# A state-space scan and four gated experts on one core: all tokens in four blocks of six chunks, each with fifteen products for eighteen

## The chip, the cores and the metric

The kernel runs on one core of a Trainium2 chip. A core has TensorE (called PE in the profile; its weight loads are PEld), VectorE (DVE), ScalarE (ACT), GpSimd (POOL) and SyncE (SP), whose queue issues nearly all transfers here. The metric is the time of one execution on the device in microseconds (us); the time before is the median of three runs, 623.88 us (623.67 to 624.11). A profile is one further execution, and its span is what the profiler saw between the first and the last instruction.

## The reference, cut to what matters

Two parts follow one another. The first is a chunked scan with a decaying state for 4 sequences of 768 tokens with 8 heads; the second mixes four experts (each two matrix products with a ReLU between) by gates per token.

```python
# first part, per sequence and head (C, B: 16 states; x: 32 values)
cum = np.cumsum(log_a_chunk)
L = np.exp(cum[:, None] - cum[None, :]) * causal
y = (C @ B.T * L) @ x + (C @ state) * np.exp(cum)[:, None]
state = np.exp(sum(log_a_chunk)) * state + (B * decay_from_j).T @ x
# bridge: y of all heads side by side gives 3072 tokens x 256
# second part
p = domain_probs / domain_probs.sum(-1, keepdims=True)
for e in range(4):
    h = np.maximum(x @ w1[e], 0.0)      # w1[e]: 256 x 1024
    out += p[:, e:e + 1] * (h @ w2[e])  # w2[e]: 1024 x 256
```

All is in 32-bit floats. The second part is most of the work.

## The kernel before, in words

The 3072 tokens are 24 chunks of 128. The first part turns each pair of chunks into a tile `yT` (features down, 256 tokens across, two halves of 128 features). The hidden units are 16 slices `fb` of 256, four to each expert. In the second part the unit of work on TensorE is a *product* (`product`, L860): two matmuls of 128x128 weights against 128x256 values, added up in half a PSUM bank or across its two halves. Done plainly, one slice and one pair of chunks take two products in the first layer and two in the second.

The kernel spares products by the family of schemes known from fast matrix multiplication: sums of weights times sums of tokens. Two are in the code, as tables at L301 to L326. `B` treats two weight slices and two pairs of chunks (a block of four chunks) with seven products for eight in each layer (`twos_first`, L1004). `H` treats three slices and three pairs (a block of six chunks) with fifteen products for eighteen (`threes_first`, L1038); as 16 slices are five groups of three and one over, one slice in a block of six is done plainly. `ORDER` (L326) lists the blocks: three of `B`, two of `H`. In block 0 the four slices of the first expert are done plainly in the first layer, so that work can start before sums exist.

What a saved product costs elsewhere:
- Sums of weights, `operands` (L920): raw slices come from HBM into W tiles; additions at L955 (DVE or POOL) make the sums, which L960 also stores in `w_d`, so that a later block reloads them (L952) instead of adding again.
- Sums of tokens, `token_sums` (L964): 256-wide additions on DVE into Y tiles.
- Between the layers: `snap` (ScalarE copies a bank to a V tile), `seed` (ScalarE copies a V tile into a bank, on which PE then adds up), `combine` (L885, an addition on DVE, or on POOL where both inputs are in SBUF) and `gated` (L896, DVE: ReLU and gate in one instruction). `threes_right` (L1080) and `twos_right` make the right-hand sums for the second layer.
- The second layer, `second` and `visit`, adds up its products in "houses", half banks that keep their sums from unit to unit: seeded, added to, copied out (L1124). At the end of a block `result` (L1159) adds them into the output, `leave` stores it.

A *unit* of the program is one group of slices (three for `H`, two pairs of slices for `B`). Its first-layer products are interleaved one for one (`put`) with the second-layer products of the unit before it (`behind`). Into this line the first part of the next block's chunks is set: scores (L472), scans of decays (`decays`, L748), outputs (L796) and `carry`, at the places that `PAIRS_AT` names, "s1" for the scores of pair 1, "o12" for the outputs of pairs 1 and 2.

The instruction order of TensorE is thus given by hand. The order on all other engines is made by a small list scheduler in the file, `Plan.run` (L181). It knows a nominal duration for each operation (`D512`, `D256` and literals), gives each a latest time from its users on TensorE, picks per engine what is ready and most urgent, chooses between DVE and POOL for additions (`BACK`, `SLACK`), keeps buffers back for urgent work (`KEEP`) and decides which buffer of a kind (V, W, Y, bank ...) a value lives in. `EARLY` lists the units in which the weight sums for the blocks of six are made ahead of time, on POOL alone (`due` in `operands`), and stored. `NV` and `NW` count the V and W tiles.

Ahead of all that, up to L692, the first two chunks are worked by hand: their decays, scores, outputs, the gates, and the first weight loads.

Of the kernel before, what the change touches and what calls it, by code (L numbers as in the profile page):

```python
# [19 lines left out]
D512, D256 = .64, .36  # L20
LANDING = 2.2
KEEP = 5
NV, NW = 31, 28
SLACK, BACK, YIELD = 0.0, 3.0, 6.0
EARLY = 1, 2, 3, 4, 5, 6, 7, 8, 9, 10
SOFT = 1
ROUND = 0, 3, 2, 0, 4
RATE, MARGIN = 330.0, 2.0
AFTER = 1
HOLD = 12.0  # L30
# [4 lines left out]
SCORED = 4  # L35
HELD = ("x", "w"), (5, 8), (0, 7)
# [6 lines left out]
    (3, 2): ((0, 1, "s0"), (1, 5, "s1"), (1, 24, "o01")),  # L43
    (4, 2): ((0, 1, "s0"), (2, 1, "s1"), (2, 14, "o01")),
    (4, 3): ((0, 1, "s0"), (0, 14, "o0"), (1, 1, "s1"), (2, 1, "s2"), (2, 14, "o12")),
    (6, 3): ((0, 1, "s0"), (0, 14, "o0"), (2, 1, "s1"), (3, 1, "s2"), (3, 14, "o12")),
# [28 lines left out]
class Plan:  # L75
# [105 lines left out]
    def run(self, line, at, begin):  # L181
# [19 lines left out]
        while todo:  # L201
# [4 lines left out]
            for w in waiting[e]:  # L206
                if w.start is not None or e == "PE" and w.place != head:
                    continue
                ready = max([w.ready, w.after.nominal + late if w.after else 0.0] + [
                    n.end + (MARGIN if n.kb and e != "SP" else -n.lag if n.by == e == "PE" else HOP)  # L210
                    for n in w.needs])
                if len(w.on) > 1 and e == "POOL":
                    if max(ready, now) + w.on[e] > w.latest + late + SLACK or self.backlog(
                            waiting["DVE"], now, t["DVE"], w) < BACK:
                        continue
                rank = w.latest
                if e == "DVE" and w.two and self.port > now + 0.05:
                    rank += YIELD
                if best is not None and ready <= now and rank >= best[0]:
                    continue  # L220
                when, homes = self.homed(
                    w, max(now, ready, self.port if e == "POOL" and w.port else 0.0))
                if when is None:
                    continue
                if when <= now + 0.02:
                    if best is None or rank < best[0]:
                        if e == "DVE" and w.two:
                            when = max(when, self.port)
                        best = rank, w, when, homes
                else:  # L230
                    if e == "DVE" and when <= now + NEAR and now < FIRST and (near is None or rank < near[0]):
                        near = rank, when
                    if soon is None or when < soon:
                        soon = when
# [79 lines left out]
H.houses = ((13, 2), (11, 4), (0, 7), (1, 14), (6, 9), (5, 8), (10, 12), (3,), ("x", "w"))  # L314
H.plain = {(0, 0): 7, (1, 0): 0, (1, 1): 8, (1, 2): 5, (0, 1): "x", (0, 2): "w"}
# [9 lines left out]
B.houses = ((1, 2), (3, 7), (5, 6), (4,))  # L325
ORDER = B, B, B, H, H  # L326
# [9 lines left out]
def kernel(  # L336
# [188 lines left out]
    a_sb = const.tile([NCH * NH // 2, 2, P], FP32, name="a_sb")  # L525
# [59 lines left out]
    a_cut = const.tile([NCH * NH // 2, 2, P], FP32, name="a_cut")  # L585
# [45 lines left out]
    gs = some(2, [P, NT, P], "gs")  # L631
# [93 lines left out]
    aq = plan.taken("V", NV - 2, 0.0)  # L725
    for c, i in ((2, 2), (3, 3)):
        st[c]["xb"] = plan.taken("xb", i, now)
# [192 lines left out]
    def operands(k, scheme, fbs, l, after=None, due=None, loaded=()):  # L920
# [3 lines left out]
        for f, fb in enumerate(fbs):  # L924
            v = loaded[f] if loaded else value("W")
            used = {x[1] for r, x in scheme.blocks[l].items() if x[0] == f and r != "b"}
            if loaded:
                pass
            elif len(used) == 1 and (*fbs, l, 0) in w_d:
# [229 lines left out]
    def result(k):  # L1159
# [3 lines left out]
        def acc(r):  # L1163
            for house in scheme.houses:
                if r in house:
                    v, i = kept.get((k, (r,)), kept.get((k, house))), house.index(r)
                    return v, lambda: whole(v)[:, i * FB:i * FB + FB]
# [22 lines left out]
        if scheme is B:  # L1190
            u, u7, u5, _ = pieces(2)
# [4 lines left out]
                     (0, 1): (acc(3), 1, u5), (1, 1): (acc(5), 1, u7)}  # L1196
        else:
# [90 lines left out]
    twos = [tuple(fbs[i:i + 2]) for i in range(0, EPB, 2)]  # L1288
    for two in twos:
        operands(0, B, two, 2, loaded=[weights[0, fb, 2] for fb in two])  # L1290
    line.extend(second(0, [(two, {1: h[two[0], 0], 2: h[two[1], 0]}) for two in twos], [(1, 2)]))
    for c in range(4):
        carry(c)
    units, last_made = [], {}
    for k, b in enumerate(blocks):
        n = E if b.scheme is B else NG
        lead = ROUND[k]
        for g in [*range(lead, n), *range(lead)]:
            if b.scheme is B and (k or g):
                units.append((k, [(4 * g + i, 4 * g + i + 1) for i in (0, 2)]))  # L1300
            elif b.scheme is H:
                units.append((k, [(3 * g + 1, 3 * g + 2, 3 * g + 3)]))
        if b.scheme is H:
            units.append((k, None))
# [14 lines left out]
    for fb in fbs:  # L1319
        first[fb, 1], h[fb, 1] = plain_first(0, fb, 1)  # L1320
    line.extend(x for fb in fbs for x in first[fb, 1])
    token_sums(0)
    right = [(two, {r: v for r, v in twos_right({
        (f, n): h[fb, n] for f, fb in enumerate(two) for n in range(2)}).items() if r > 2}) for two in twos]
    behind = second(0, right, B.houses)
# [3 lines left out]
    for u, (k, groups) in enumerate(units):  # L1329
# [28 lines left out]
        else:  # L1358
            held = [(fbs, right(h)) for fbs, (_, h) in zip(groups, made)], b.scheme.houses
# [8 lines left out]
        if k < len(blocks) - 1:  # L1368
            for unit, x, what in PAIRS_AT[len(of_block), blocks[k + 1].scheme.pairs]:
# [13 lines left out]
                at[x] = line[mark:]  # L1383
# [58 lines left out]
```

## Time and profile before

| what | value |
|---|---|
| median of 3 runs | 623.88 us (623.67 to 624.11) |
| the profiled execution | 624.43 us, of which its span 622.5 us |
| PE busy | 617.0 us (99%), 3435 records |
| PEld busy | 528.5 us (85%) |
| DVE busy | 531.3 us (85%), 883 instructions |
| ACT busy | 268.3 us (43%), 568 |
| POOL busy | 172.3 us (28%), 199 |
| DMA | 126.65 MB, mean 203 GB/s |

How to read it: an engine's busy time is what its instructions cover, and says nothing yet about who waits for whom. A row of forty digits cuts the span into equal slices, each digit the busy share in tenths. The chain follows the last instruction back to what released it, again and again, to the start; an engine with a large share of it sets the time. A group line names the source line, engine, operation, the tiles by the program's names, how often, then busy time and the mean of one in ns, then the engine's idle time before those instructions and what ended it. Each fp32 matmul of the program leaves two records. A query by stretches gives busy time and counts of each engine between two moments of the span.

### The profile page before, as it was taken

The numbers are of one execution on the slowest core, as the hardware profiler recorded it, in microseconds if no ns is written. First come the engines' busy times: TensorE is split into PE (matmuls) and PEld (weight loads), VectorE is DVE, ScalarE is ACT, GpSimd is POOL, SyncE is SP. The second block draws the span as 40 slices with busy tenths as digits, with TensorE's granted clock in tenths as the row PEclk, the third lists the DMA queues.
The fourth block names the chain that finished last, engine by engine and source line by source line (L and its number), as shares of the span: only waits on it lengthen the run. The fifth ranks groups of instructions, "written<-read, shape, count | busy, mean of one in ns | idle before, by whom it ended". The sixth has DMA issues, their size and how long they took to land.

```text
span 622.5 us, 10250 instructions
## 1 busy us (share of the span) xinstructions
PE 617.0 (99%) x3435; PEld 528.5 (85%) x3435; DVE 531.3 (85%) x883; ACT 268.3 (43%) x568; POOL 172.3 (28%) x199
## 2 busy tenths in 40 slices
PE   9999999999999999999999999999999999999997
PEld 5888888888888888888888888888888888888886
DVE  7999999997968799789689999959797987869684
ACT  4242464422356343236534336445443344555441
POOL 4637644840527654156350000100000000000000
PEclk9999999999999999999999999999999999999999
DMA  7999489673898878399999737535131424943001
GB/s 253 330 298 359 152 273 276 231 247 88 271 341 291 284 227 264 63 332 322 346 352 292 249 79 255 180 117 178 59 110 52 138 40 122 376 130 111 0 1 51
DMA packets 112307, 126.65 MB, mean 203 GB/s; under 512 B 28916, under 2 KB 78336, under 8 KB 112256
## 3 DMA queue, kind: packets, MB, share of 16 engines
q1 hardware_dynamic: 112100, 125.96, 63.0%
q8 instruction: 27, 0.44, 0.3%
q14 instruction: 24, 0.20, 0.1%
q10 hardware_dynamic: 156, 0.06, 0.0%
HBM read 101.09 MB, written 24.89 MB: 202 GB/s over the span
## 4 chain that ended last, share of the span: by engine, by line
PE 98%; DVE 1%; ACT 0%; issue 0%; DVEq 0%; ACTq 0%
PE bank L864 91%; PE bank L505 2%; PE bank L472 2%; DVE LT L489 1%; PE bank L810 1%; PE bank L644 1%; DVE MT L788 0%; PE bank L620 0%; PE bank L1245 0%; PE bank L612 0%; ACT A L515 0%; ACT v L687 0%; DVE v L1176 0%; ACT v L1250 0%; DVE v L899 0%
## 5 line engine op out<-in xcount | busy, mean ns | idle before, releaser
L864 PE MATMUL bank<-v,w 128*128 128x256 f32 x1856 | 436.6, 380 | 0.0
L864 PEld LDWEIGHTS bank<-v,w 128*128 128x128 f32 x1856 | 351.1, 190 | 51.9 <-issue 3.6
L891 DVE TENSOR_TENSOR v<-v,v 128x512 f32<-128x512 f32 x267 | 196.6, 765 | 16.2 <-ACT v L873 13.5
L864 PE MATMUL bank<-Y,w 128*128 128x256 f32 x792 | 203.3, 379 | 0.0
L864 PEld LDWEIGHTS bank<-Y,w 128*128 128x128 f32 x792 | 150.3, 190 | 20.9 <-issue 0.6
L899 DVE SCALAR_TENSOR_TENSOR v<-bank,gate 128x512 f32<-128x512 f32 x172 | 116.8, 684 | 34.9 <-PE bank L864 30.2
L878 ACT COPY bank<-v 128x512 f32<-128x512 f32 (+1 forms) x195 | 109.0, 571 | 64.4 <-DVE v L891 42.6
L955 POOL TENSOR_TENSOR w<-w,w 128x256 f32<-128x256 f32 x102 | 100.5, 1008 | 55.4 <-PE bank L864 19.6
L873 ACT COPY v<-bank 128x512 f32<-128x512 f32 x106 | 62.0, 585 | 109.3 <-PE bank L864 108.9
L1124 ACT COPY v<-bank 128x512 f32<-128x512 f32 x105 | 61.5, 585 | 96.2 <-PE bank L864 95.0
L891 POOL TENSOR_TENSOR v<-v,v 128x512 f32<-128x512 f32 x11 | 15.6, 1414 | 247.2 <-DVE v L891 192.6
L489 DVE TENSOR_TENSOR_SCAN LT<-ab,ident 128x512 f32<-128x512 f32 x42 | 53.0, 1276 | 0.4 <-DMA ab<-acut_d 0.4
L891 DVE TENSOR_TENSOR v<-bank,v 128x512 f32<-128x512 f32 x40 | 27.6, 689 | 9.1 <-PE bank L864 8.9
L499 POOL TENSOR_TENSOR MT<-xb,LT 128x64 f32<-128x64 f32 (+1 forms) x28 | 16.3, 586 | 42.5 <-DVE LT L489 31.5
L773 POOL TENSOR_TENSOR cts<-ctm,dec 128x256 f32<-128x256 f32 x20 | 17.6, 892 | 37.0 <-ACT ctm L465 24.5
L788 DVE TENSOR_TENSOR MT<-bank,LT 128x512 f32<-128x512 f32 x44 | 27.3, 681 | 0.1
L1127 ACT COPY v<-bank 128x256 f32<-128x256 f32 x22 | 8.2, 372 | 37.8 <-PE bank L864 33.9
L1176 DVE TENSOR_TENSOR v<-v,v 128x256 f32<-128x256 f32 x52 | 20.3, 420 | 4.0 <-ACT v L1124 3.9
L465 ACT ACTIVATE ctm<-xb,tmask 128x128 f32<-128x128 f32 x48 | 16.4, 394 | 15.0 <-DMA xb<-in_xbc_dram 15.0
L1026 DVE TENSOR_TENSOR bank<-bank,v 128x512 f32<-128x512 f32 x22 | 15.2, 693 | 5.2 <-PE bank L864 5.0
L955 POOL TENSOR_TENSOR w<-w 128x256 f32<-128x256 f32 x14 | 14.1, 1008 | 11.8 <-DMA w<-in_w_dram 6.9
L955 DVE TENSOR_TENSOR w<-w,w 128x256 f32<-128x256 f32 x36 | 14.9, 443 | 0.0
(71 smaller groups left out, 202.5 us busy)
## 6 DMA issues: line engine op xcount, KB each, us to landing
w<-w_d SPq DMA_DIRECT2D x134, 256.0 KB
w<-in_w_dram SPq DMA_DIRECT2D x128, 256.0 KB
w_d<-w SPq DMA_DIRECT2D x82, 256.0 KB
ab<-acut_d SPq DMA_DIRECT2D x21, 512.0 KB
w<-in_w_dram SPq DMA_DIRECT2D x40, 128.0 KB
gate<-p_d SPq DMA_DIRECT2D x10, 384.0 KB
xb<-in_xbc_dram SPq DMA_DIRECT2D x17, 192.0 KB
gate<-p_d SPq DMA_DIRECT2D x11, 256.0 KB
```

Of the source, the lines that this page charges most:

```text
L465: nc.scalar.mul(ctm[:, t], xb[:, OCT:OCT + P], tmask[:, t:t + 1])
L489: nc.vector.tensor_tensor_scan(out=LT.rearrange("p h s -> p (h s)")[:, lo:lo + w], data0=src, data1=ident.rearrange("p h s -> p (h s)")[:, ...
L773: plan.add({"POOL": .72}, lambda e: nc.gpsimd.tensor_mul(s["cts"].t, s["ctm"].t, s["dec"].t.unsqueeze(1).to_broadcast([HN, NT, P])), reads ...
L788: nc.vector.tensor_mul(s["MT"].t[:, js, h, 0:P], g, s["LT"].t[:, js, h])
L864: nc.tensor.matmul(out=o, lhsT=w[:, j], rhs=x if half is None else x[:, j], start=(start and j == 0), stop=(j == 1), skip_group_check=True)
L873: act(.5, lambda e: nc.scalar.copy(out=flat(v), in_=bank.t), reads=[bank], writes=[v])
L878: act(.54 if to - lo > FB else .32, lambda e: nc.scalar.copy(out=bank.t[:, lo:to], in_=flat(v)[:, lo:to]), reads=[v], writes=[bank])
L891: plan.add(engines, lambda e: (on(e).tensor_add if sign > 0 else on(e).tensor_sub)(flat(v), whole(x), whole(y)), reads=[x, y], writes=[v], ...
L899: dve(D512, lambda e: nc.vector.scalar_tensor_tensor(out=h.t, in0=whole(x).rearrange("p (j m) -> p j m", j=JJ), scalar=0.0, in1=g.t[:, 2 * ...
L955: plan.add({"POOL": .72} if due else B256, lambda e, r=r, x=x, y=y, sign=sign: (on(e).tensor_add if sign > 0 else on(e).tensor_sub)(view(r ...
L1124: act(.5, lambda e: nc.scalar.copy(out=flat(v), in_=bank.t), reads=[bank], writes=[v])
L1176: plan.add(engines, lambda e: (on(e).tensor_add if sign > 0 else on(e).tensor_sub)(o[1](), x[1](), y[1]()), reads=[v for v in vs if v is n ...
```

## The change

All 24 chunks now go by the scheme `H`: `ORDER` is four blocks of six. With no block of four left, the weight sums can't be made during one: `EARLY` is empty, and each group's sums are made when block 0 (for one group: block 1) first uses the group, on DVE or POOL, and stored; later blocks reload them.

Block 0 begins otherwise. The slices of the first expert are done plainly in both layers and for all three pairs: the first layer of pair 0, its second layer (house (0, 7)), the first layer of pair 1, its second layer (house (8, "x")), with the scores and outputs of chunks 4 and 5 set into and behind these, then pair 2, whose second layer (5, "w") is interleaved with the first unit. Block 0 has then four groups and no plain unit of its own. Its houses are paired a little differently (`first_houses`), which `acc` in `result` takes account of.

Around it: other nominal durations and thresholds for the scheduler, 34 V tiles for 31 and 27 W tiles for 28; the tiles of `a` and of two early score copies (`gs`) are laid into a V and a W tile that are not yet in use; other places in `PAIRS_AT`; the order of groups in a block (`ROUND`); POOL takes no choice additions before 30 us of planned time (`EASY`).

```diff
-D512, D256 = .64, .36
+D512, D256 = .60, .34
-KEEP = 5
-NV, NW = 31, 28
-SLACK, BACK, YIELD = 0.0, 3.0, 6.0
-EARLY = 1, 2, 3, 4, 5, 6, 7, 8, 9, 10
+KEEP = 7
+NV, NW = 34, 27
+SLACK, BACK, YIELD = 0.0, 2.0, 6.0
+EARLY = ()
-ROUND = 0, 3, 2, 0, 4
+ROUND = 0, 4, 3, 2
-HOLD = 12.0
+HOLD = 6.0
+EASY = 30.0
+FOURS = 4
...
-    (4, 3): ((0, 1, "s0"), (0, 14, "o0"), (1, 1, "s1"), (2, 1, "s2"), (2, 14, "o12")),
-    (6, 3): ((0, 1, "s0"), (0, 14, "o0"), (2, 1, "s1"), (3, 1, "s2"), (3, 14, "o12")),
+    (4, 3): ((0, 1, "s0"), (0, 14, "o0"), (1, 1, "s1"), (1, 14, "o1"), (2, 1, "s2"), (2, 14, "o2")),
+    (6, 3): ((0, 1, "s0"), (2, 1, "o0"), (2, 1, "s1"), (3, 1, "s2"), (3, 23, "o12")),
...
-                            waiting["DVE"], now, t["DVE"], w) < BACK:
+                            waiting["DVE"], now, t["DVE"], w) < (BACK if now > EASY else 99):
...
+H.first_houses = ((13, 2), (11, 4), (0, 7), (1, 14), (6, 9), (8, "x"), (5, "w"), (10, 12), (3,))
...
-ORDER = B, B, B, H, H
+ORDER = H, H, H, H
...
-    a_sb = const.tile([NCH * NH // 2, 2, P], FP32, name="a_sb")
+    a_sb, a_cut = (homes["V"][-4][:NCH * NH // 2, i].rearrange("p (r s) -> p r s", r=2) for i in range(2))
...
-    gs = some(2, [P, NT, P], "gs")
+    gs = [homes["W"][-1][:, NT * P * i:NT * P * (i + 1)].rearrange("p (t s) -> p t s", t=NT) for i in range(2)]
...
-    twos = [tuple(fbs[i:i + 2]) for i in range(0, EPB, 2)]
-    for two in twos:
-        operands(0, B, two, 2, loaded=[weights[0, fb, 2] for fb in two])
-    line.extend(second(0, [(two, {1: h[two[0], 0], 2: h[two[1], 0]}) for two in twos], [(1, 2)]))
+    line.extend(visit(0, (0, 7), plain_terms(0, fbs, h, [(0, 0), (1, 0)])))
     for c in range(4):
         carry(c)
+    dma(lambda e: nc.sync.dma_start(
+        out=g0.t[:, 4:6], in_=p_d[0, 4:6].rearrange("c s -> (c s)").partition_broadcast(P).rearrange(
+            "p (c s) -> p c s", s=P)), 1, 128, part=[g0])
+    for c in (4, 5):
+        fetch(c)
+        decays(c)
+    for fb in fbs:
+        first[fb, 1], h[fb, 1] = plain_first(0, fb, 1)
+    begun = [x for fb in fbs for x in first[fb, 1]]
+    line.extend(begun[:FOURS])
+    scores([4, 5])
+    line.extend(begun[FOURS:])
+    line.extend(visit(0, (8, "x"), plain_terms(0, fbs, h, [(1, 1), (0, 1)])))
+    outputs([4, 5])
+    for c in (4, 5):
+        carry(c)
...
-        first[fb, 1], h[fb, 1] = plain_first(0, fb, 1)
-    line.extend(x for fb in fbs for x in first[fb, 1])
+        first[fb, 2], h[fb, 2] = plain_first(0, fb, 2)
+    line.extend(x for fb in fbs for x in first[fb, 2])
     token_sums(0)
-    right = [(two, {r: v for r, v in twos_right({
-        (f, n): h[fb, n] for f, fb in enumerate(two) for n in range(2)}).items() if r > 2}) for two in twos]
-    behind = second(0, right, B.houses)
+    behind = visit(0, (5, "w"), plain_terms(0, fbs, h, [(1, 2), (0, 2)]))
```

Left out of this copy: the loss of the argument `loaded` in `operands`, what the scheme `B` would need as a first block (it isn't used any more), the new `acc`, the note of when the two borrowed tiles come free, and that two things may stand at one place of `PAIRS_AT`.

## The prediction

> **What bounds the kernel now.** I read the page from the top, then the chain, then stages cut at the points where the chain passes a score matmul (L472), then single stretches of the timeline. First the page of before: busy times, the slices, the chain's shares, and the groups that matter.
>
> ```profile
> span 622.5 us, 10250 instructions
> ...
> PE   9999999999999999999999999999999999999997
> ...
> DVE  7999999997968799789689999959797987869684
> ...
> POOL 4637644840527654156350000100000000000000
> ...
> PE 98%; DVE 1%; ACT 0%; issue 0%; DVEq 0%; ACTq 0%
> ...
> L864 PE MATMUL bank<-v,w 128*128 128x256 f32 x1856 | 436.6, 380 | 0.0
> ...
> L864 PE MATMUL bank<-Y,w 128*128 128x256 f32 x792 | 203.3, 379 | 0.0
> ...
> L955 POOL TENSOR_TENSOR w<-w,w 128x256 f32<-128x256 f32 x102 | 100.5, 1008 | 55.4 <-PE bank L864 19.6
> ```
>
> TensorE (PE) is busy in every slice and holds 98% of the chain; its two product groups show no idle time before them. So time goes with the number of products while nothing makes PE wait. But VectorE (DVE) is nearly as full in many slices: it is the next bound.
>
> The chain in order of time gives the price of a product. Columns: start, length, what.
>
> ```profile
> 34.35 1.08 PE bank L472 x16
> 35.43 24.37 PE bank L864 x112
> ```
>
> 112 matmul records in 24.37 us are 0.218 us each; the longest piece of the chain (924 in 199.63 us) gives 0.216. A program matmul leaves two records and a product is two program matmuls, so a product costs 4 x 0.216 = 0.865 us.
>
> Now the stages between score matmuls (columns: stretch, length, then busy time and count of PE, weight loads, DVE, ACT, POOL, then clock, DMA share, GB/s).
>
> ```profile
> 34.35:59.80 25.45, 25.45 (x133) 21.92 (x132) 25.16 (x43) 9.77 (x19) 13.60 (x12) 1.00 0.98 327
> 59.80:108.92 49.12, 49.12 (x324) 42.20 (x324) 47.54 (x86) 24.34 (x58) 24.73 (x29) 1.00 0.74 237
> 108.92:158.54 49.62, 49.62 (x245) 43.20 (x244) 44.54 (x69) 17.59 (x32) 19.88 (x23) 1.00 0.57 180
> ...
> 317.35:371.47 54.12, 54.12 (x305) 46.47 (x304) 51.45 (x86) 21.63 (x48) 6.97 (x8) 1.00 0.71 225
> 371.47:398.64 27.17, 27.17 (x140) 23.44 (x140) 26.01 (x40) 13.24 (x25) 1.59 (x1) 1.00 0.70 227
> ...
> 413.68:615.69 202.01, 202.01 (x940) 177.83 (x940) 164.57 (x284) 92.05 (x176) 3.83 (x3) 1.00 0.35 106
> ```
>
> The reader is to see two kinds of stage in which DVE is 95% or more full and PE still never waits: the early one, where POOL works half the time, and the first block of six (317 to 399), where POOL hardly works. The changed kernel puts the two on top of each other.
>
> [...] Timeline of before, six alike DVE additions with POOL at work and six without:
>
> ```profile
> 83.10 5.12 POOL L955 TENSOR_TENSOR w<-w,w 128x256 f32<-128x256 f32 x5 [0.18 <-PE bank L864]
> ...
> 85.83 4.97 DVE L891 TENSOR_TENSOR v<-v,v 128x512 f32<-128x512 f32 x6
> ...
> 490.57 3.69 DVE L891 TENSOR_TENSOR v<-v,v 128x512 f32<-128x512 f32 x6
> ```
>
> 4.97 against 3.69: the trace agrees that they hinder each other (1.28 us lost to about five POOL operations), though both still progress. I price by the measured loss.
>
> **The change, part by part.**
>
> *Products.* Counted from the instruction orders of both kernels: L864 has 1324 program matmuls before (its 2648 records are twice that), and the same line has 1308 after. By hand: before 114+112+112+162+162 = 662 products, after 168+162+162+162 = 654. Eight fewer, 8 x 0.865 = **-6.9 us**, on the path. Every other matmul line has the same count in both orders.
>
> *Spacing of DVE work.* Start to start without POOL: a 512-wide operation 3.61/6 = 0.60 (490.57 to 494.18), 256-wide 0.34 (two of L955 from 78.73 to 79.40), a decay scan of 512 1.13 (101.41 to 102.54), a dec scan 0.40, a state update 0.6. I count each kernel's DVE instructions between consecutive score products and multiply. Before: the three early stages need 21.9, 41.9 and 38.5, were busy 25.16, 47.54 and 44.54, in sum 14.9 more, with 58.2 us of POOL beside them: 0.25 us lost per busy POOL us (single stages 0.23 to 0.30). The check: 317 to 371 needs 50.1 and was busy 51.45 with 6.97 of POOL.
>
> *Block 0 after.* Plain column pairs, then four groups of fifteen. Between the scores of chunks 4,5 and those of 12,13, PE's own work is 127.8 us (by 0.435 a matmul, and scores, outputs as in the chain). DVE's need by the same counts is 19.9+21.9+27.0+50.7 = 119.5. POOL has some 43 sums of weights (1.008), 8 L773 (0.892), 7 additions of 512 (1.414) and 12 L499 (0.6) there: 67.5 us. At 0.25 that costs DVE 16.9, so DVE needs 136.4 against 127.8: **8.6 us too much**. With 0.20 it is 5.2, with 0.30 12. Of the 32 additions and gates of a group, 13 (threes_right) feed second-layer products which come one unit, about 26 us, later; they can slip, 13 x 0.60 = 7.8 us of work in any unit, as far as the V buffers allow (34 instead of 31). So most of the excess becomes a backlog rather than a wait; gates and seeds of the first layer can't slip. Below nothing it can't go, since PE has no wait here to lose; above, all 8.6 falls on PE. I take a quarter, **+2.1**, with first-unit seeds as the likeliest place: a score multiplication and a scan stand on DVE ahead of the subtraction of product 12, which ScalarE then copies to a bank that PE wants.
>
> *A new wait.* The output matmuls of chunks 4,5 are directly followed by plain products on those outputs. PE's first matmul there waits for ScalarE's copy of chunk 5. Nearest row: the same step of chunk 1.
>
> ```profile
> 12.00 0.51 ACT L687 COPY v<-bank 128x128 f32<-128x128 f32 x2 [0.32 <-PE bank L505]
> ...
> 12.77 0.30 PEld L864 LDWEIGHTS bank<-v,w 128*128 128x128 f32 x2 [0.33 <-ACT v L687]
> ```
>
> 0.32 to the copy, 0.38 for a 128x256 copy (L825 has 376 ns), 0.26 until the weight load: **+1.0 us**, and all queued PE work stands behind it. Between 0.7 and 1.5. Before, eight other products lay at the like place.
>
> *Blocks 1 to 3.* Block 1 makes the last twenty sums: DVE needs 133.8 plus some 11 for 44 us of POOL, against 144.2 of PE. Even, so a backlog isn't worked off there. Blocks 2 and 3 make no sums and are like before's stages from 317 on, where PE never waited: 56.5+24.9 against 87.4, then 163.5 against 222. Nothing added.
>
> *What moves without a price.* Sums fall from 164 to 100 (POOL 116 to 56, DVE 48 to 44) and no longer run ahead of their users: in before POOL did the hundred for the blocks of six long before their use. In block 0 a late one stops PE; each has more than a unit, and is in the excess above. Transfers shrink: 256 KB weight loads 128 to 88, reloads of sums 134 to 110, stores 82 to 50, half loads 40 to 22, gates about equal: some 27 MB less of 126.65. SP's queue is 558 rows against 674; in block 0 it brings six raw tiles per 26 us plus chunks, less than the 327 GB/s of before's fullest early stage. ScalarE gets 29 instructions more (43% busy): hidden. The a rows and the score copies now live in a V and a W buffer that are wanted only after they are free. One W home less: a group takes 16, two groups overlap as in before's blocks of six. The planner's constants (durations nearer to the 0.60 and 0.34 above, KEEP, BACK, HOLD, EASY) add no instruction of their own; what they do to the order is in the counts, which are of the order as it comes out. The end of the program has the same six result transposes.
>
> **Sum**, against the profiled execution (span 622.5, 624.43 with 1.93 around it): 622.5 - 6.9 + 1.0 + 2.1 = 618.7, with the 1.93, 620.6. The median of the runs shown is 0.55 below that execution, so **620.1**.
>
> **Rivals.**
> - *The backlog hides all.* DVE is 96% full in 371.47:398.64 with no PE wait, which speaks for a planner that copes; there POOL was quiet, which speaks against. 624.43 - 6.9 + 1.0 - 0.55 = 618.0, or 617.0 without the new wait.
> - *A wash.* Waits of 5.7 to 8.2 eat the gain: half or more of the excess on PE and the first-unit seeds late by a few us. 622.6 to 625.1, middle 623.9.
> - *Slower: [...].* All the excess falls on PE: 623.88 - 6.9 + 1.0 + 8.6 = 626.6; with 0.30 of loss 630. It decides from 8.2 us of waits up. For it: early DVE at 97 to 99% already with only 86% of need. Against: the slip above, and that POOL takes additions off DVE.
> - *Fewer products not real.* Excluded by the counts.
>
> **How the numbers follow.** Forecast case (waits of 1.6 to 5.7, 618.5 to 622.6) 0.42; all hidden 0.27; wash 0.13; slower 0.18. Faster by over 0.2% means below 622.6, slower above 625.1; 0.2% is about what a measurement here can tell from no change. Faster 0.69, same 0.13, slower 0.18. The range runs from 616.9, the bare eight products, to 626.0, which leaves out the worst of the slower case.
>
> **What would show it.** Right: 2616 records of the product line; a PE gap near 1 us behind the outputs of chunks 4,5, released by the ScalarE copy; PE gaps behind "ACT bank" copies or DVE between 45 and 170 us that sum to about 2; DVE at 97% or more there, v,v additions of 850 ns or more; no gaps after 230 us. Wrong: PE gaps above 6 us in sum, PE waiting for POOL's sums or for DMA, or gaps in blocks 2 and 3.

## The result, and the profile after

The changed kernel takes 627.36 us (median; 627.14 to 627.42), the kernel before beside it 624.0: a ratio of 1.0051, 95% interval 1.0031 to 1.0071. It is slower by about half a per cent, where 620.1 was forecast. The first profiled execution of the changed kernel was disturbed (2278 us, its matmul records 0.82 us apart for 0.216), so the profile shown is that of a repeat.

In theory 1 below VectorE and GpSimd hinder each other in block 0.

> The changed kernel as it is, for a profile in which PE runs at its usual pace. Theory 1 ([...]): PE idle of 8 to 11 us in sum, nearly all between 45 and 230 us, ended by VectorE or by ScalarE copies that waited for VectorE; VectorE 97% busy or more there. Theory 2 (weight sums or transfers come late): the same sum, but ended by GpSimd sums or DMA. Theory 3 (single waits in the new start, in the hand-written line): most of the idle before 60 us.

The repeat took 627.5 us (626.75 to 629.79), ratio 1.0045 (1.0028 to 1.0062). Its profiled execution, at 629.79 us, is the slowest of the four. In it a transfer came 2.0 us late for a scan on VectorE, and TensorE waits 2.0 us at 23.7 us for the score multiplications behind that scan; a wait of over 1 us there is found in three of the eleven profiles of kernels with this start. The page of the repeat, lines as shown of before; line numbers are those of the changed kernel: L869 is a product, L896 `combine`, L904 `gated`, L883 `seed`, L793 a score multiplication, L1178 an addition of `result`, L958 a sum of weights (in runs whose edit adds lines, the numbers are some lines higher):

```profile
span 628.0 us, 10010 instructions
...
PE   9999999999999999999999999999999999999997
...
DVE  6899999999999999999999989968796977869684
...
PE 56%; DVE 7%; DMA 1%; issue 1%; ACT 1%; DVEq 0%; ACTq 0%
...
L896 DVE TENSOR_TENSOR v<-v,v 128x512 f32<-128x512 f32 x276 | 196.9, 746 | 14.3 <-ACT v L878 13.4
...
L896 POOL TENSOR_TENSOR v<-v,v 128x512 f32<-128x512 f32 x28 | 43.3, 1554 | 234.8 <-DVE v L896 137.8
...
L958 POOL TENSOR_TENSOR w<-w,w 128x256 f32<-128x256 f32 x48 | 42.9, 910 | 36.3 <-PE bank L869 25.8
```

The products went as counted. But VectorE's row is now 9 from the third slice to about 360 us without a break (its additions of 512 columns take 0.75 us in the mean, much as the 0.77 of before; GpSimd's take 1.55), and the chain that ended last is no longer TensorE's alone: 56% for 98%. Here is that chain where it leaves TensorE for VectorE, in block 1, shortly behind the sums that end block 0 (columns: start, length, what):

```profile
...
223.23 0.60 DVE v L904
223.83 0.60 DVE v L896
224.43 2.25 DVE LT L493 x2
226.69 0.59 DVE v L904
227.28 0.04 issue
227.32 7.82 PE bank L869 x35
```

A gate (L904) that a product needs stands behind two scans of decays for the next block's chunks, and ahead of those the chain shows the same engine at work without a gap from 217.41 us on. Now the waits of TensorE over the whole repeat (who waited for whom: sum, times, longest), where before's list has only the start's 0.8 and 0.4:

```profile
PE bank L509 <- DVE MT L793: 2.0, 1, 2.0
PE bank L869 <- ACT bank L883: 1.9, 3, 1.4
PE bank L869 <- DVE v L896: 1.3, 3, 0.6
PE bank L476 <- ACT v L830: 1.0, 1, 1.0
PE bank L647 <- PEq L1451: 0.8, 1, 0.8
PE bank L869 <- DVE v L904: 0.7, 1, 0.7
PE bank L869 <- DVE MT L793: 0.5, 1, 0.5
PE bank L869 <- ACT v L830: 0.5, 1, 0.5
...
```

The list comes to 9.0 us. The 2.0 is the start wait. The rest is small and scattered. The stages between score matmuls show where it adds up (columns as in the prediction):

```profile
35.94:57.81 21.87, 21.38 (x152) 17.59 (x152) 21.30 (x40) 3.26 (x10) 10.11 (x14) 1.00 0.92 298
57.81:81.42 23.61, 23.31 (x160) 19.02 (x160) 23.50 (x39) 8.90 (x24) 9.07 (x14) 1.00 0.74 243
81.42:111.30 29.88, 29.34 (x188) 24.34 (x188) 29.84 (x47) 15.14 (x32) 19.14 (x20) 1.00 0.55 182
111.30:167.26 55.96, 55.71 (x308) 46.97 (x308) 55.93 (x91) 31.89 (x68) 25.65 (x26) 1.00 0.53 176
167.26:223.28 56.02, 55.03 (x304) 47.14 (x305) 54.58 (x92) 24.08 (x48) 31.72 (x30) 1.00 0.31 91
223.28:252.60 29.32, 28.05 (x140) 23.61 (x140) 29.06 (x44) 14.72 (x30) 11.08 (x10) 1.00 0.64 192
252.60:314.36 61.76, 61.76 (x381) 52.96 (x380) 60.97 (x103) 31.96 (x73) 9.04 (x11) 1.00 0.68 227
314.36:376.27 61.91, 60.49 (x332) 51.71 (x332) 59.26 (x105) 23.26 (x46) 10.58 (x9) 1.00 0.35 99
376.27:403.87 27.60, 27.41 (x140) 23.33 (x140) 26.49 (x41) 16.38 (x38) 4.69 (x3) 1.00 0.82 266
```

Set against TensorE's own work in the forecast, the sums by block are:

| stretch | TensorE's own | took | lost | VectorE busy | POOL busy |
|---|---|---|---|---|---|
| block 0 (first four lines) | 127.8 | 131.3 | 3.5 | 130.6 | 64.0 |
| block 1 (next three) | 144.2 | 147.1 | 2.9 | 144.6 | 51.8 |
| block 2 (last two) | 87.4 | 89.5 | 2.1 | 85.8 | 15.3 |
| behind block 2, 403.80 to the end | 223.9 | 224.2 | 0.3 | | |

In the last line the 223.9 is what the kernel before took from the same scores to its end (398.57 to 622.50 us, with the same 1117 records); the forecast's 222 was TensorE's work alone, without the 3.6 us at the end in which only other engines work. Block 0 lost 3.5 us, near the 3.1 of the forecast. The rest, 5.3 us, was forecast at nothing. The repeat's span lies 9.3 us above the forecast's 618.7: 0.4 of it in block 0, these 5.3, and 1.6 ahead of the first line (35.94 us for 34.35). The last 2.0 are in the forecast's own sums: its stage figures, with the start and the end of before, come to 617.6 us, where its sum began with 622.5 - 6.9 = 615.6 (the stages were reckoned with 0.435 us a matmul; the records show 0.432). So the loss of one block is known to about 1 us only.

### The profile page after: what moved, and what is told of

The parts are those of the page before. It is cut to its first block, busy times and chain, and to the rows that moved or that the text cites. A ratio compares the mean times of both kernels' runs of the same rounds, so it can differ in the third digit from the quotient of the medians.

```text
span 2276.5 us, 10010 instructions
## 1 busy us (share of the span) xinstructions
PE 2270.6 (100%) x3403; PEld 1200.0 (53%) x3403; DVE 566.9 (25%) x953; ACT 285.1 (13%) x597; POOL 132.8 (6%) x169
## 4 chain that ended last, share of the span: by engine, by line
PE 65%; ACT 0%; issue 0%
PE bank L869 64%; PE bank L509 1%; PE bank L476 1%; PE bank L815 0%; PE bank L1250 0%; ACT v L1255 0%; ACT v L830 0%; ACT A L519 0%
## 5 line engine op out<-in xcount | busy, mean ns | idle before, releaser
L869 PE MATMUL bank<-v,w 128*128 128x256 f32 x1780 | 1526.4, 1107 | 0.5 <-ACT v L830 0.5
L869 PEld LDWEIGHTS bank<-v,w 128*128 128x128 f32 x1780 | 773.0, 435 | 685.9 <-issue 671.2
L869 PE MATMUL bank<-Y,w 128*128 128x256 f32 x836 | 744.1, 1096 | 0.0
L869 PEld LDWEIGHTS bank<-Y,w 128*128 128x128 f32 x836 | 369.8, 442 | 316.4 <-issue 304.7
L904 DVE SCALAR_TENSOR_TENSOR v<-bank,gate 128x512 f32<-128x512 f32 x154 | 105.2, 689 | 681.7 <-PE bank L869 647.3
L896 DVE TENSOR_TENSOR v<-v,v 128x512 f32<-128x512 f32 x276 | 188.2, 716 | 84.0 <-ACT v L878 83.0
L896 DVE TENSOR_TENSOR v<-bank,v 128x512 f32<-128x512 f32 x76 | 52.6, 692 | 600.7 <-PE bank L869 596.1
L883 ACT COPY bank<-v 128x512 f32<-128x512 f32 (+1 forms) x222 | 124.4, 575 | 292.1 <-DVE v L896 210.5
L896 POOL TENSOR_TENSOR v<-v,v 128x512 f32<-128x512 f32 x28 | 39.4, 1414 | 969.9 <-DVE v L896 553.0
L958 POOL TENSOR_TENSOR w<-w,w 128x256 f32<-128x256 f32 x48 | 36.9, 783 | 292.5 <-PE bank L869 232.3
L793 DVE TENSOR_TENSOR MT<-bank,LT 128x512 f32<-128x512 f32 x44 | 27.4, 683 | 69.5 <-PE bank L476 69.5
L509 PE MATMUL bank<-MT,xb 128*32 128x144 f32 (+1 forms) x384 | 44.3, 710 | 0.0
L476 PE MATMUL bank<-ctm,xb 32*128 32x256 f32 x192 | 42.1, 1055 | 1.4 <-ACT v L830 0.9
L1178 DVE TENSOR_TENSOR v<-v,v 128x256 f32<-128x256 f32 x65 | 26.1, 435 | 66.2 <-ACT v L1127 62.6
L509 PEld LDWEIGHTS bank<-MT,xb 128*32 128x32 f32 x384 | 27.6, 209 | 20.9 <-issue 17.9
```

Of the source, the lines that this page charges most:

```text
L476: nc.tensor.matmul(out=views[r][:, j], lhsT=xb[j][k, OBT:OBT + P], rhs=ctm[j][k].rearrange("p t s -> p (t s)"), start=(j == 0), stop=True, ...
L509: nc.tensor.matmul(out=y[32 * q:32 * q + 32, 0:w], lhsT=xb[:, h * D:h * D + D], rhs=MT[:, place(c, NT * q + t), 0:w], start=start, stop=Tr ...
L793: nc.vector.tensor_mul(s["MT"].t[:, js, h, 0:P], g, s["LT"].t[:, js, h])
L869: nc.tensor.matmul(out=o, lhsT=w[:, j], rhs=x if half is None else x[:, j], start=(start and j == 0), stop=(j == 1), skip_group_check=True)
L883: act(.54 if to - lo > FB else .32, lambda e: nc.scalar.copy(out=bank.t[:, lo:to], in_=flat(v)[:, lo:to]), reads=[v], writes=[bank])
L896: plan.add(engines, lambda e: (on(e).tensor_add if sign > 0 else on(e).tensor_sub)(flat(v), whole(x), whole(y)), reads=[x, y], writes=[v], ...
```

## The experiments

The theory after the result: VectorE is full from block 0 to block 2, and most of the waits above go back to it; of the time lost, what VectorE loses to GpSimd's reads of SBUF is the larger part. The rivals: VectorE simply has too many instructions; the planner's new constants order the work badly; the waits belong to the places at which the scores and outputs are set into the line; the kernel before loses as much time to GpSimd, and the gain went elsewhere. Differences in us are those of two ratios to the kernel before, times its 624; by the intervals of the ratios, each is known to 1 to 1.5 us.

**Fewer additions.** Three of the thirteen right-hand sums of each group are left out (57 additions less in all, 52 of them on VectorE), so the output is another one.

```diff
-        T[2] = combine(n10, n12)
+        T[2] = n10
-        T[11] = combine(p, n10, reuse=False)
+        T[11] = p
-        T[14] = combine(h[0, 0], h[0, 2])
+        T[14] = h[0, 0]
```

> The changed kernel without three of the thirteen right-hand additions of each group (sums 2, 11 and 14 of the second layer are replaced by one of their terms, so the output is another). Theory A (VectorE's time, with what it loses to GpSimd, is the bound through blocks 0 to 2): some 57 additions of 0.60 us less, about 1.8 us in each unit of 26 us, more than the 10 us that PE waits; PE waits shrink to 3 us or less, 618 to 620 us. Theory B (PE waits at fixed places of the hand-written line, whatever VectorE's load): 625 to 627.5.

Measured: 626.63 us (626.32 to 627.68), ratio 1.0041 (1.0026 to 1.0056): nothing gained that the intervals can tell. The stretches 81 to 167 and 167 to 250 us of this kernel, and then of the repeat:

```profile
81.00:167.00 86.00, 84.57 (x489) 71.31 (x488) 85.79 (x138) 46.74 (x100) 38.44 (x41) 1.00 0.54 179
167.00:250.00 83.00, 80.93 (x424) 69.67 (x422) 81.29 (x136) 39.03 (x78) 32.26 (x33) 1.00 0.42 129
```

```profile
81.00:167.00 86.00, 85.21 (x490) 71.33 (x488) 85.94 (x137) 47.03 (x100) 45.21 (x45) 1.00 0.54 179
167.00:250.00 83.00, 80.74 (x431) 68.83 (x430) 81.30 (x132) 38.44 (x76) 42.19 (x38) 1.00 0.41 119
```

VectorE is as full as in the repeat in both (85.79 for 85.94, 81.29 for 81.30) with about as many instructions; it is GpSimd whose busy time fell, by 7 and 10 us. The planner gives freed VectorE time to additions that GpSimd had. Later VectorE does get room (58.49 us busy for 63.21 between 250 and 314 us), but there the repeat's TensorE doesn't wait. So the run doesn't test the count as it was meant to: in the stretches shown, taking work off VectorE takes it off GpSimd.

**GpSimd's additions read nothing.** Same order on TensorE and VectorE; each of GpSimd's 101 additions becomes two fills of the same tile, which take somewhat less time (0.62 us for a 256-wide addition's 0.91, 1.05 for a 512-wide one's 1.55). The sums are not made. GpSimd's 48 multiplications for scores and outputs still read. Theory A below has two forms: VectorE loses its time to GpSimd's reads (618 to 621 us), or to the mere number of its own instructions. (The edit, shortened; the same at the other two places where additions are made.)

```diff
-                    on(e).tensor_add if sign > 0 else on(e).tensor_sub)(view(r), view(x), view(y)),
+                    blank(view(r)) if e == "POOL" else (as before)
...
+    def blank(t):
+        nc.gpsimd.memset(t, 0.0)
+        nc.gpsimd.memset(t, 0.0)
```

> The changed kernel in its order, but each addition that GpSimd makes (sums of weights, additions of V tiles) is two memsets of the same tile, so GpSimd keeps its place and nearly its time but reads no SBUF; the output is another. Theory A [...]: VectorE's additions come down from 800 to about 690 ns in the first 220 us, VectorE gets back 10 us or more, 618 to 621 us. Theory A [...] (the mere number of VectorE operations): 625 to 627.5. If late GpSimd sums were the cause, the same 618 to 621 but with VectorE's additions as slow as before.

Measured: 621.94 us (621.53 to 622.94), ratio 0.9962 (0.9951 to 0.9974): 5.2 us less than the changed kernel, a little above the 618 to 621 of the theory that GpSimd's reads take it from VectorE. The same stretches:

```profile
81.00:167.00 86.00, 86.00 (x499) 73.37 (x498) 80.58 (x140) 47.89 (x102) 30.45 (x81) 1.00 0.56 182
167.00:250.00 83.00, 81.16 (x433) 69.13 (x432) 75.88 (x132) 37.04 (x75) 28.27 (x61) 1.00 0.44 131
```

As many VectorE instructions take 5.4 us less in each, and TensorE never waits in the first. VectorE's 512-wide additions of two V tiles came down from 0.814 to 0.685 us in the mean (both from 36 to 167 us); with no GpSimd at work they take 0.680 (ten of them, 490 to 500 us of the kernel before), so beside the fills nearly nothing is lost. The fills are shorter than the additions, so their tiles are also there earlier; but in the repeat TensorE never waits for GpSimd, and VectorE once, for 0.9 us. What changed for VectorE is that GpSimd's additions no longer read beside it.

**The same on the kernel before.** The control: does it lose time to GpSimd's reads too? Theory A: little, as its VectorE isn't full where GpSimd is busy; theory B: as much as the changed kernel. Only the kernel differs, the edit is that of the run above.

> The kernel before with the same edit as the run in which GpSimd only writes: every addition of GpSimd is two fills that read nothing from SBUF (the output is not the reference's). Theory A, [...]: 623-624.3, a gain of 0 to 1 us against 5.6 us for the changed one. Theory B, [...] and the change lost its gain elsewhere: 619-621.

Measured: 623.04 us (622.75 to 625.36), ratio 0.9985 (0.9976 to 0.9994): 0.9 us. VectorE's busy time falls as much as in the changed kernel, by 23.8 us (531.3 to 507.5) against 24.6 (564.6 to 540.0), for 131 additions and 101. So GpSimd takes as much from VectorE in both kernels; before, VectorE had room for it, and TensorE's waits were 1.2 us in all. Some 4.3 us of the cost came with the change.

**Only the weights' sums as fills.** Of the replacement above, only that of the 56 weight sums. Theory A has nearly all of the cost in block 0.

> The changed kernel, with only the 56 weight sums that GpSimd makes in block 0 as fills that read nothing; GpSimd's other additions stay. Theory A, [...]: nearly all of the 5.6 us comes back, 621.5-623. Theory B, the cost is spread over blocks 0 to 2 by the additions of products: 624-626, that is 1.5 to 3 us come back, and the waits from 210 to 320 us remain.

Measured: 626.04 us (625.37 to 626.71), ratio 1.0020 (1.0013 to 1.0027): 1.6 us back, at the edge of theory B. The other 3.6 belong, by difference, to GpSimd's additions of products and outputs. Those tripled with the change: 15 before (the groups of 11 and of 4 in the first fence, from the kernel before), 45 after (28 and 17, second fence, from the page of the repeat; count, then busy time, mean in ns):

```profile
L891 POOL TENSOR_TENSOR v<-v,v 128x512 f32<-128x512 f32 x11 | 15.6, 1414 | 247.2 <-DVE v L891 192.6 <-ACT bank L878 53.7 <-DVE v L899 0.9
...
L1176 POOL TENSOR_TENSOR v<-v,v 128x256 f32<-128x256 f32 x4 | 3.1, 774 | 26.9 <-ACT v L1124 26.9
```

```profile
L896 POOL TENSOR_TENSOR v<-v,v 128x512 f32<-128x512 f32 x28 | 43.3, 1554 | 234.8 <-DVE v L896 137.8
...
L1178 POOL TENSOR_TENSOR v<-v,v 128x256 f32<-128x256 f32 x17 | 15.1, 906 | 39.5 <-DVE v L1178 20.2
```

Of the 45, seven fall in block 0, 23 in block 1, seven in block 2 and eight behind it.

**Fewer additions at the block ends.** 13 additions stand in for the 23 of `result` in blocks 0 to 2 (the expectations say 11 and "12 of 23", which is a miscount: the traces have 62 of them for 92), so the output is another one.

```diff
-            chain(g1, acc(13), (-1, acc(9)))
-            chain(p12, g1, (1, acc(2)), (-1, acc(11)), (1, acc(14)))
... (six more chains)
+            few() if k < len(blocks) - 1 else full()
+            # few: p00 = acc(1) + acc(6) + acc(3), and one addition for each of five others
```

> At the end of blocks 0 to 2, 11 additions of products stand in for the 23 of the scheme (the six pieces of the output are then not the right ones). Theory A, the burst of VectorE work at a block's end is what makes the waits of products 200 to 330 (3.4 + 1.6 us over the kernel before): 12 additions of about 0.7 us per block end go, the waits at 216 to 250 us and at 310 to 320 us close, and the time falls by 3 to 5 us, to 622.5-624.5. Theory B, VectorE is full everywhere and the planner moves other additions from GpSimd to it as soon as it has room: GpSimd's busy time falls instead, and the time stays at 626-627.5.

Measured: 624.79 us (623.58 to 625.39), ratio 0.9999 (0.9991 to 1.0008), just above the range of theory A: 2.9 us less, for 30 additions of 256, where 57 of 512 left out evenly gained nothing. The additions of a block's end come at once, together with the transposes, the scans and the gates of the next block; time given back there is time that products wait for. (That it is their coming at once, and not the planner's other order with fewer of them, is argued; the stages below show where the time came back.)

**All of these together.** Fills on GpSimd, three right-hand sums fewer, short block ends. In theory A their gains add up (5.2 and 2.9 us), in theory B they overlap.

> Three edits of earlier runs together: GpSimd's additions read nothing, three of thirteen right-hand additions are left out in each group, and 12 of 23 additions at the end of each of blocks 0 to 2 (outputs are not the reference's). Theory A, all that the changed kernel lost but the turns and waits fixed by its written line is VectorE's lateness: [...], 618-620 us, with waits left only behind the outputs of chunks 4 and 5 (47 us) and before the scores right behind outputs (about 219 us). Theory B, the two overlap, because a VectorE relieved by one of them is no longer late: 620.5-622, [...].

Measured: 619.78 us (618.95 to 620.47), ratio 0.9926 (0.9909 to 0.9943), 7.4 us less than the changed kernel and 4.6 less than the kernel before. Its waits of TensorE:

```profile
PE bank L873 <- DVE v L900: 0.9, 1, 0.9
PE bank L647 <- PEq L1469: 0.8, 1, 0.8
PE bank L873 <- ACT v L834: 0.5, 1, 0.5
...
```

What is left behind the start's 0.8 are mainly one late addition and the copy behind the outputs of chunks 4 and 5. So with VectorE relieved 4.6 of the 6.9 us that the products save come out. That the forecast's ratio (620.1 to 623.88, 0.9939) lies within the interval confirms nothing: the forecast had 2.1 us of waits for VectorE in it, which this run was to take away. The single gains, 5.2, 2.9 and 0.2, sum to 8.3; the difference to 7.4 is within their uncertainty. Where each gain lies, in us from scores to scores:

| kernel | block 0 | block 1 | block 2 | behind |
|---|---|---|---|---|
| the repeat | 131.3 | 147.1 | 89.5 | 224.2 |
| weight sums as fills | 129.8 | 147.0 | 89.5 | 224.2 |
| all GpSimd's additions as fills | 129.5 | 146.2 | 87.2 | 223.4 |
| short block ends | 131.0 | 145.5 | 88.1 | 224.2 |
| all together | 129.8 | 144.4 | 87.3 | 223.4 |

The sums of weights cost block 0 alone; what GpSimd's other additions cost lies nearly all behind it.

**The new constants.** The planner's constants as in the kernel before, all else changed.

```diff
-D512, D256 = .60, .34
+D512, D256 = .64, .36
-KEEP = 7
+KEEP = 5
-SLACK, BACK, YIELD = 0.0, 2.0, 6.0
+SLACK, BACK, YIELD = 0.0, 3.0, 6.0
-HOLD = 6.0
+HOLD = 12.0
-EASY = 30.0
+EASY = 0.0
```

> The changed kernel with the scheduler's constants of the kernel before (D512 .64, D256 .36, KEEP 5, BACK 3, HOLD 12, no EASY). Theory A: the load is the same, so 626 to 630 us. If the new constants are what costs the time: 620 to 623.

Measured: 633.76 us (632.8 to 635.15), ratio 1.0154 (1.0138 to 1.0169), 6.8 us more, above both ranges. The new constants as a whole are no cause of the loss; they save more than the 3 us by which the changed kernel is slower. (They also change the load: GpSimd makes 85 additions here, not 101.)

**All sums of weights on VectorE.** The other way round: GpSimd's 56 sums are done on VectorE, which GpSimd then hinders less (its additions of two V tiles take 0.72 us in the mean for the repeat's 0.75).

```diff
-                plan.add({"POOL": .72} if due else B256, lambda e, r=r, x=x, y=y, sign=sign: (
+                plan.add({"POOL": .72} if due else {"DVE": D256}, lambda e, r=r, x=x, y=y, sign=sign: (
```

> The changed kernel with all 100 sums of weights on VectorE. Theory A: VectorE gets 56 x 0.34 = 19 us more in blocks 0 and 1 and is spared about 0.2 us for each of some 50 us of GpSimd, in sum 9 us more on the bound: 632 to 637 us. If VectorE has hidden room (theory B): 626 to 629.

Measured: 638.19 us (637.34 to 638.49), ratio 1.0221 (1.0205 to 1.0236), 11 us more, a little above the range of theory A. Its two longest waits, 4.4 and 3.4 us, end at 221 and 234 us, shortly behind the sums that end block 0 (TensorE's list of waits, first two lines):

```profile
PE bank L869 <- DVE v L896: 6.3, 3, 4.4
PE bank L869 <- DVE v L904: 3.4, 1, 3.4
...
```

56 sums at about 0.34 us are, by estimate, 19 us of VectorE, and what they cost on GpSimd was 1.6 us of time by the run with fills: making them on GpSimd is still much the cheaper way.

**The places of the outputs.** In the repeat the scores at 223.28 us wait 1.24 us longer than their turn, for ScalarE's copy of outputs that stand right before them. First these outputs were set ten products earlier:

```diff
-    (6, 3): ((0, 1, "s0"), (2, 1, "o0"), (2, 1, "s1"), (3, 1, "s2"), (3, 23, "o12")),
+    (6, 3): ((0, 1, "s0"), (1, 20, "o0"), (2, 1, "s1"), (3, 1, "s2"), (3, 23, "o12")),
```

> The first outputs of the next block stand ten products ahead of its second scores instead of right before them. Theory A, the 1.24 us wait of those scores for the copy of the outputs (at 223.28 us of the changed kernel's repeat), and its like at the two other block changes, is the neighbourhood alone: it goes, [...], and the time falls by 1 to 2 us, to 625.5-626.5. Theory B, the wait only stands for a VectorE that is late there: another wait of VectorE takes its place within 20 us, and the time stays at 626.8-628.

Measured: 631.58 us (630.35 to 633.93), ratio 1.0110 (1.0091 to 1.0129), 4.1 us more, above both ranges. The wait for the copy is gone, and between 205 and 260 us TensorE now waits five times for VectorE (list of waits of that stretch):

```profile
PE bank L869 <- DVE v L896: 4.6, 4, 1.9
PE bank L476 <- DVE v L904: 1.2, 1, 1.2
```

Then they were set 13 products later:

```diff
-    (6, 3): ((0, 1, "s0"), (2, 1, "o0"), (2, 1, "s1"), (3, 1, "s2"), (3, 23, "o12")),
+    (6, 3): ((0, 1, "s0"), (2, 1, "s1"), (2, 14, "o0"), (3, 1, "s2"), (3, 23, "o12")),
```

> The first outputs of the next block stand 13 products behind its second scores instead of right before them, a real kernel. Theory A, VectorE is behind at the end of each block, and work that the outputs bring with them costs most there: moving them ten products ahead cost 4.2 us, so moving them 13 behind gains, by the 1.24 us of the scores' wait and some of the 0.86 and 0.73 us behind it: 624.5-626.5. Theory B, any other order than this one costs, since the planner's order around it is a lucky one: 628-632, as in the run with them ahead.

Measured: 631.25 us (630.13 to 632.18), ratio 1.0113 (1.0095 to 1.0131), 4.2 us more. My reading of the run before, that earlier is worse and so later is better, fell with it: both ways are worse.

**Small shifts of order.** Two constants and two places, which lie in the units of block 0 (the expectation names block 2 by mistake). Theory B has the losses go with the counts and with what GpSimd takes from VectorE.

```diff
-SLACK, BACK, YIELD = 0.0, 2.0, 6.0
+SLACK, BACK, YIELD = 0.0, 2.5, 6.0
-HOLD = 6.0
+HOLD = 8.0
-    (4, 3): ((0, 1, "s0"), (0, 14, "o0"), (1, 1, "s1"), (1, 14, "o1"), (2, 1, "s2"), (2, 14, "o2")),
+    (4, 3): ((0, 1, "s0"), (0, 14, "o0"), (1, 4, "s1"), (1, 14, "o1"), (2, 1, "s2"), (2, 18, "o2")),
```

> Two of the planner's constants (2.0 to 2.5 us, 6 to 8 us) and two places of the line around block 2's end changed: a real kernel. Theory A, the kernel is so full on VectorE that small shifts of order move some microseconds either way without a cause in the work: 624 to 631. Theory B, [...]: 626.5-628.5.

Measured: 633.41 us (632.35 to 634.89), ratio 1.0150 (1.0131 to 1.0169), 6.6 us more, a little outside the wider range. The counts are not quite the same as in the repeat: in the three kernels with shifted places GpSimd makes 93 to 98 additions for 101. With so little changed in the load, order moves 4 to 7 us. The outputs set earlier, the small shifts and the old constants lost most between products 200 and 260, around the end of block 0 and the start of block 1; the outputs set later lost about half there, the rest soon after and around the end of block 2. No full kernel of these runs beats the kernel before.

## Why the prediction was wrong, point by point

- *Products, -6.9 us*: right. The line left 2616 records (1780 and 836), 32 fewer, 0.216 us apart; with VectorE relieved the kernel is 4.6 us faster than the one before.
- *Spacing of VectorE's work, 0.25 us lost per busy us of GpSimd*: right as a size, as a mean over whole blocks. With the forecast's needs (119.5, 133.8 and 56.5 + 24.9) the measured busy times give a loss of (130.6 - 119.5) / 64.0 = 0.17 in block 0, (144.6 - 133.8) / 51.8 = 0.21 in block 1, (85.8 - 81.4) / 15.3 = 0.29 in block 2.
- *Block 0, +2.1, and the new wait, +1.0*: right in sum, 3.5 measured against 3.1, with its parts off in opposite directions. GpSimd's work there was 64.0 us for 67.5 forecast. The new wait is at 49.75 us, as the timeline of the repeat has it, 0.49 where 0.7 to 1.5 was allowed, so about 3.0 are left for VectorE:

```profile
47.48 0.66 PE L815 MATMUL bank<-cts,S 32*32 32x256 f32 x16
48.07 1.19 PE L509 MATMUL bank<-MT,xb 128*32 128x144 f32 x32
49.75 2.43 PE L869 MATMUL bank<-v,w 128*128 128x256 f32 x10 [0.49 <-ACT v L830]
```

- *Blocks 1 to 3, "Nothing added"*: this is the step that failed. In the repeat they lost 5.3 us (2.9, 2.1 and 0.3); the relieved kernel is 2.7, 2.2 and 0.8 us shorter there. For block 1 the forecast itself had 133.8 plus 11 against TensorE's 144.2 and called it even; measured were 144.6, so the sum was right, and 2.9 us were lost all the same. An engine that is even with TensorE over a block can be behind it in parts of the block: the work of a block's end comes together (2.9 us came back when 30 of these additions went), and gates queue behind scans, as in the chain above. For block 2 I took before's stages from 317 us on as the model, where TensorE never waited at 95 and 96% of VectorE; but there GpSimd had 7.0 and 1.6 us of work, here 10.6 and 4.7. How one such meeting comes about is in the repeat's timeline at 314 us, here in short windows so that the additions stand singly:

```profile
313.94 1.27 POOL L896 TENSOR_TENSOR v<-v,v 128x512 f32<-128x512 f32 x1 [1.23 <-DVE v L896]
...
314.38 1.37 DVE L896 TENSOR_TENSOR v<-v,v 128x512 f32<-128x512 f32 x1
...
315.17 1.72 POOL L896 TENSOR_TENSOR v<-v,v 128x512 f32<-128x512 f32 x1
...
315.68 1.75 DVE L896 TENSOR_TENSOR v<-v,v 128x512 f32<-128x512 f32 x1
...
317.35 2.47 DVE L793 TENSOR_TENSOR MT<-bank,LT 128x512 f32<-128x512 f32 x4
```

Two additions of each engine take turns. GpSimd's first takes the 1.27 us of an addition alone (the shortest of its 28). VectorE's first, begun in the meantime, ends 0.54 us after it; GpSimd's second ends 1.14 us after that, and VectorE's second again 0.54 us after GpSimd's second. So VectorE's two take 3.05 us, where two take 1.2 with GpSimd quiet. Then come four score multiplications that stand ahead; a seed on ScalarE waits for the first of them, and TensorE's product at 318.76 waits 1.42 us for the seed. Behind block 2 it is the same: two additions of VectorE from 404.38 us on take 2.36 us beside two of GpSimd, a score multiplication follows, and a product waits 0.52 us for it. With all of GpSimd's additions as fills both waits are gone.
- *What moves without a price*: GpSimd's sums of weights fell from 116 to 56 as counted, but its additions of products and outputs rose from 15 to 45, of which the forecast names the seven in block 0, but none of the 38 later ones. By the fills, the 45 cost 3.6 us of the 5.2. That what the constants do to the order "is in the counts" was wrong as well: with nearly equal counts, order moved 4 to 7 us.
- *The slip of the right-hand sums*: not shown either way. The run with fewer of them gained nothing, but the planner had given the room away.
- *The rival "All the excess falls on PE"* gave 626.6, near the measured 627.4 by luck: it put 8.6 us into block 0, which lost 3.5. The hindrance of VectorE by GpSimd is real and costs 4.3 us more than in the kernel before, but most of it lies behind block 0.
- *"Both still progress"* was a misreading. Of the forecast's six additions in 4.97 us three take the usual 0.68 and three are late (1.21, 1.21 and 0.90 us). Each of these three ends 0.54 or 0.55 us behind an operation of GpSimd that was at work when it began: GpSimd's run from 85.86 to 87.10, 87.06 to 88.23 and 88.19 to 89.05 us, VectorE's from 86.43 to 87.64, 87.56 to 88.77 and 88.70 to 89.60. These are the turns of 314 us again, with the same 0.54. With fills in place of GpSimd's additions VectorE's time in 81 to 167 us fell by 5.4 us for the same work. What makes the two wait for each other isn't shown. The 0.25 us lost per busy us of GpSimd is a mean over additions that meet and others that don't, and says nothing of where they meet.

"PE gaps above 6 us in sum" and "gaps in blocks 2 and 3" had been named as what would show the forecast wrong, and did. Of its other signs, VectorE above 97% in block 0 came true (130.6 of 131.3 us), additions of 850 ns or more did not (813 ns between 81 and 167 us). What stays open: why this one order loses less than its neighbours, since the planner's order changes in many places at once; and what the relieved kernel still lacks of the 6.9 us beyond its listed waits (0.9, 0.5 and some shorter ones).

## What to carry to other kernels

When a change makes a second engine as full as the first, a sum per stage that comes out even is no zero: price the stage's ends, where that engine's work comes at once, and count the work of an engine that hinders it (here 0.17 to 0.29 us lost per busy us of GpSimd) in every stage and of every kind. Leaving work out is a weak test of fullness where a scheduler balances two engines, as it gives the room away; taking the hindrance away at equal order (here writes instead of reads) showed it, and the stages of that run showed where. And test the suspected cost on the kernel before as well: it lost as much of VectorE's time there (23.8 us for 24.6), but only 0.9 us of the kernel's for 5.2.

## What the hardware showed unasked

In the run with the outputs set ten products earlier, a wait of TensorE is followed by products at half speed. Stretches of it before, in and behind (columns as above; the clock is the third number from the end):

```profile
248.00:251.20 3.20, 1.28 (x7) 0.79 (x5) 3.20 (x6) 0.63 (x2) 1.13 (x2) 1.00 1.07 358
251.20:254.60 3.40, 3.40 (x8) 2.69 (x9) 3.15 (x6) 0.54 (x1) 0.33 (x1) 0.52 1.07 367
254.60:256.00 1.40, 1.40 (x8) 1.21 (x7) 0.35 (x2) 0.86 (x2) 0.40 (x1) 0.95 1.06 377
```

Eight records from 251.18 to 254.64 us take 0.43 us each instead of 0.216, 1.7 us more in sum, behind a wait of 1.92 us. The granted clock is 0.52 in the second stretch and 0.95 in the third, which makes about 3.4 us at half clock, by estimate (0.96 of 3.40 us and 0.10 of 1.40). With the old constants the clock is 0.51 from 218.00 to 221.40 us and 0.50 from there to 224.90, about 6.8 us by the same estimate; with the sums on VectorE it is 0.50 from 221.40 to 224.00 us and again from 231.00 to 237.60. Little work of TensorE ahead isn't enough to bring this about: in the first stretch above it was busy for 1.28 of 3.20 us, but with the small shifts for 1.27 of the 3.40 us from 317.80 on, and there the mean clock of the whole execution is 0.999, where one such fall leaves 0.997 (the run with the outputs earlier). What brings the clock down, these runs don't show.
